# Top-32 attention and two rational/cosine layers: the mask moved to ScalarE, two elementwise steps moved to VectorE

## The chip, the cores and the metric

The kernel runs on one core of a Trainium2 chip. The metric is the device time of one execution in microseconds (us). TensorE multiplies matrices, VectorE, ScalarE and GpSimd work elementwise, SyncE issues transfers. In profile rows TensorE is PE (its weight loads PEld), VectorE is DVE, ScalarE ACT, GpSimd POOL, SyncE SP.

## The reference, cut to what matters

Attention with 4 batches, 8 heads, 576 positions and 64 features per head. Of each row of scores only the 32 largest are kept. Then two layers over 2304 tokens (512 wide, 2048 inside) follow, the first with a rational function, the second with h cos(h). All is in float32.

```
kth  = 32nd largest of the row of scores
attn = exp(where(scores >= kth, scores, -1e9) - max)
attn = attn / (sum(attn) + 1e-9);  x = attn @ v
h = x @ w_in                                # first layer
P = a0 + a1 h + a2 h^2 + a3 h^3;  Q = 1 + |b0| |h| + |b1| h^2
x = (P / (Q + 1e-6)) @ w_out
h = x @ w_in2;  out = (h * cos(h)) @ w_out2 # second layer
```

## The kernel before, in words

**Units.** Attention is cut into 72 units: 18 query tiles of 128 rows times 4 pairs of heads. `qk(i)` multiplies queries by keys on TensorE into the PSUM tile `sx` and ScalarE copies the scores of both heads to SBUF (`sS`, two buffers). `topk(i)` finds the 32 largest on VectorE: it folds each row into element-wise maxima and minima of its two halves (tile `e`, two buffers), then takes eight maxima at a time (`hd`, MAX8) and strikes them out (MATCH_REPLACE8), four rounds in all, the first two on the maxima alone. ScalarE scales the negated row maximum (`nb`), and forms exp(SCALE * score + nb) for all scores, into `e`. Last, VectorE multiplies by the mask score >= hd[31] and sums the row as it goes, the sum into `sums`. `av(i)` transposes `e` on TensorE (tiles `pp`, copied to SBUF as `pt` by ScalarE) and multiplies by the values; `norm` scales by the reciprocal sums once four units of a tile are done.

**Matrix stages.** The tokens come in 9 blocks of 256; block k needs the 8 units of query tiles 2k and 2k+1. Each of the two layers has 8 groups per block, 72 in all. `in1` multiplies by the first weights (`mm_in`, into PSUM tile `h`), copies to `w`, and starts the rational function on ScalarE and GpSimd: `u` = -(a3 w + a2) on ScalarE, then u * w on GpSimd. `mid1` and `end1` finish on VectorE, `out1` multiplies by the second weights into `y`. For the second layer `in2` copies `h` to `hs`, forms `rr` = hs/2pi + 1/4, adds the constant MAGIC (which rounds to an integer, into `n`, a tile on the single buffer "ob" that the output rows also use), subtracts to get the fraction, and takes the sine of two groups in one ScalarE instruction. The sine needs another activation table than the exponential and the logarithm, so a table is loaded before and after it. `mul2` and `out2` follow. Operands are split in a high and a low part, so that each product is three multiplications. The weights are converted and split in the first part of the run (`conv`), among the attention.

**Order.** `attention()` is a generator of five pieces per unit. A loop over pieces starts it and calls the matrix stages' functions at piece numbers worked out ahead (`timed`). The framework then orders the instructions of each engine with a simulated timeline, tied by a window of pieces for VectorE, ScalarE and GpSimd (`Windowed`, line 70), up to piece 150, 90 and 90. On the chip each engine works in that order. Nearly all elementwise instructions are issued through `Windowed`, so their line in the profile is L79, and the tile's name tells them apart. The PSUM pools for `h`, `y`, `o` and the transposes have one buffer each. `DV1` = 8 and `DV2` = 7 are the blocks from which some steps of GpSimd and ScalarE go to VectorE instead.

The lines that decide the mask's place are, in `topk`:

```
for j, s in enumerate(tiles):
    top(j, both, 3)
    A.activation(e[:, j], s, AF.Exp, bias=nb[:, j:j + 1], scale=SCALE)
yield
...
V.scalar_tensor_tensor(e[:, j], s, hd[j][:, 31:32], e[:, j],
                       op0=ALU.is_ge, op1=ALU.mult, accum_out=row)
```

In the next unit's first piece the loop takes two steps of the generator of the unit before, which are these masks, and then calls `av(i - 1)`.

Of the kernel before, what the change touches and what calls it, by code (L numbers as in the profile page):

```python
# [10 lines left out]
F32 = mybir.dt.float32  # L11
# [3 lines left out]
AF = mybir.ActivationFunctionType  # L15
ALU = mybir.AluOpType
# [7 lines left out]
P = 128  # L24
# [3 lines left out]
SCALE = 0.125  # L28
HALF = S // 2
NEG = -3.0e38  # L30
VW = 640
TWO_PI = 6.283185307179586
MAGIC = 12582912.0
SSC = TWO_PI
# [15 lines left out]
NC0 = 36  # L50
C2 = 80
PM = 150
PMASK = range(0)
WA, PA = 12, 90
WG, PG = 10, 90
N1, NU, N2, NST, NGG = 2, 2, 3, 4, 3
# [32 lines left out]
def body(tc, out, qt, kt, vt, ident_d, w1_d, w1o_d, a_d, b_d, w2_d, w2o_d):  # L89
    nc = tc.nc  # L90
    V, A, G = Windowed(tc, nc.vector, WIN, PM), Windowed(tc, nc.scalar, WA, PA), Windowed(tc, nc.gpsimd, WG, PG)
    PE, SP = nc.tensor, nc.sync

    with ExitStack() as ctx:
        def pool(name, bufs=1, **k):
            return ctx.enter_context(tc.tile_pool(name=name, bufs=bufs, **k))

        cst = pool("cst")
# [3 lines left out]
        sml = pool("sml", 4)  # L102
# [25 lines left out]
        sx = ps_s.tile([P, 2, 512], F32, name="sx")  # L128
# [51 lines left out]
        def load_v(i):  # L180
# [4 lines left out]
            for j, (b, _) in enumerate(qts[n]):  # L185
                v = kv.tile([P, VW], F32, tag="v", bufs=VB, name=f"v{i}_{b}")
                A.dma_start(out=v, in_=vt[b, pr])
# [14 lines left out]
        V.tensor_scalar_mul(nega, coef[:, 0:4], -1.0)  # L202
        quarter = cst.tile([P, 1], F32)
        G.memset(quarter, 0.25)
        magic = cst.tile([P, 1], F32)
        G.memset(magic, MAGIC)
        qc = cst.tile([P, 1], F32)
        G.memset(qc, QC)
        tc.keep_in_program_order(A.preload_act_table_set("natural_log_exp_and_others"))
        na0, na1, na2, na3 = (nega[:, i:i + 1] for i in range(4))  # L210
# [68 lines left out]
        def halves(ap):  # L279
            return ap.rearrange("p (a c) -> p a c", a=2)  # L280

        def after(mm, bank):
            for x in order[bank]:
                tc.add_manual_dep(mm.ins, x, mybir.DependencyInfo(mybir.DependencyClass.NoSync, mybir.DependencyReason.DATA), reason="bank")

        def qk(i):
            n, pr = units[i]
            raw, hi, lo = (*qpair[i // 2], None, None)[:3]
            kvs = ins[i]
            m = P // len(kvs)  # L290
            st[i] = sb = att.tile([P, 2, S], F32, tag="sS", bufs=2, name=f"sS{i}")
            for j in range(2):
                rows = slice(j * D, (j + 1) * D)
                for c, (k, _) in reversed(list(enumerate(kvs))):
                    q0 = i % 2 * P
                    qs, qc = slice(0, (c + 1) * m), slice(q0, q0 + (c + 1) * m)
                    for hf in range(2):
                        o = sx[qs, hf, :HALF]
                        hs = slice(hf * HALF, (hf + 1) * HALF)
                        if n < 2:  # L300
                            mm = PE.matmul(o, raw[rows, j, qc], k[rows, 0, hs].bitcast(F32), start=True, stop=True)
                            after(mm, hf)
                        else:
                            mm = PE.matmul(o, hi[:, j, qc], k[:, j, hs], start=True, stop=False, skip_group_check=True)
                            after(mm, hf)
                            mm = PE.matmul(o, lo[:, j, qc], k[:, j, hs], start=False, stop=True, skip_group_check=True)
                        order[hf] = [mm.ins.name]
                A.activation(halves(sb[:, j]), sx[:, :, :HALF], AF.Copy)
            if n == 1:
                store_k(kvs[0][0], 0, pr)  # L310

        def topk(i):
            n, pr = units[i]
            sc = st.pop(i)
            tiles = [sc[:, j] for j in range(2)]
            e = att.tile([P, 2, S], F32, tag="e", bufs=EB, name=f"e{i}")
            et[i] = e
            kb, t = n // 2, n % 2
            if i % 8 == 0:
                sums[kb] = sml.tile([P, 2, H], F32, tag="sum", bufs=2, name=f"sum{kb}")  # L320
            sm = sums[kb][:, t]
            hds = sml.tile([P, 2, 32], F32, tag="hd", bufs=2, name=f"hd_{i}")
            hd = [hds[:, j] for j in range(2)]
            nb = sml.tile([P, 2], F32, tag="nb", bufs=2, name=f"nb_{i}")
            big = [e[:, j, :HALF] for j in range(2)]
            both = [e[:, j] for j in range(2)]

            def top(j, x, r):
                V.max(out=hd[j][:, 8 * r:8 * r + 8], in_=x[j])

            def drop(j, x, r):
                V.match_replace(out=x[j], in_to_replace=hd[j][:, 8 * r:8 * r + 8], in_values=x[j], imm_value=NEG)

            l, r = sc[:, :, :HALF], sc[:, :, HALF:]
            V.tensor_tensor(e[:, :, :HALF], l, r, op=ALU.max)
            top(0, big, 0)
            yield
            V.tensor_tensor(e[:, :, HALF:], l, r, op=ALU.min)
            top(1, big, 0)
            A.activation(nb, hds[:, :, 0], AF.Copy, scale=-SCALE)  # L340
            yield
            for step in (((drop, big, 0), (top, big, 1)), ((drop, big, 1), (top, both, 2)), ((drop, both, 2),)):
                for f, *x in step:
                    for j in range(2):
                        f(j, *x)
                yield
            for j, s in enumerate(tiles):
                top(j, both, 3)
                A.activation(e[:, j], s, AF.Exp, bias=nb[:, j:j + 1], scale=SCALE)
            yield  # L350
            for j, s in enumerate(tiles):
                row = sm[:, 2 * pr + j:2 * pr + j + 1]
                if i in PMASK:
                    G.tensor_scalar(s, s, hd[j][:, 31:32], 1.0, op0=ALU.is_ge, op1=ALU.mult)
                    G.tensor_mul(e[:, j], e[:, j], s)
                    A.activation(s, e[:, j], AF.Copy, accum_out=row)
                else:
                    V.scalar_tensor_tensor(e[:, j], s, hd[j][:, 31:32], e[:, j], op0=ALU.is_ge, op1=ALU.mult, accum_out=row)
                yield

        def av(i):
# [89 lines left out]
        def in1(k, g):  # L451
            h = mm_in(0, k, g).rearrange("p a t -> p (a t)")
            w, q, r, u = (mo.tile([P, BT * 2], F32, tag="m1" + t, bufs=NU if t == "u" else N1, name=f"{t}{k}_{g}") for t in "wqru")
            A.activation(w, h, AF.Copy)
            A.activation(r, w, AF.Abs)
            A.activation(q, r, AF.Identity, scale=b1, bias=b0)
            E1 = V if k >= DV1 else G
            E1.tensor_mul(q, q, r)
            A.activation(r, q, AF.Ln, bias=qc)
            A.activation(r, r, AF.Exp, scale=-1.0)  # L460
            A.activation(u, w, AF.Identity, scale=na3, bias=na2)
            E1.tensor_mul(u, u, w)
            g1[k, g] = (q, r, u, w)

# [52 lines left out]
        def in2(k, g):  # L517
            h = mm_in(1, k, g).rearrange("p a t -> p (a t)")
            if g % SINB == 0:
                rp[k, g // SINB] = late[0].tile([P, SINB, 512], F32, tag="rr", bufs=2, name=f"rr{k}_{g}")  # L520
            rs = rp[k, g // SINB]
            rr = rs[:, g % SINB]
            hs = late[0].tile([P, 512], F32, tag="hs", bufs=N2, name=f"hs{k}_{g}")
            rt[k, g] = rr, hs
            A.activation(hs, h, AF.Copy)
            n = late[0].tile([P, DM], F32, tag="ob", bufs=OBB, name=f"n{k}_{g}")
            if k >= DV2:
                V.tensor_scalar(rr, hs, 1.0 / TWO_PI, 0.25, op0=ALU.mult, op1=ALU.add)
            else:
                A.activation(rr, hs, AF.Identity, scale=1.0 / TWO_PI, bias=quarter)  # L530
            A.activation(n, rr, AF.Identity, bias=magic)
            V.scalar_tensor_tensor(rr, n, MAGIC, rr, op0=ALU.subtract, op1=ALU.subtract)
            if g % SINB == SINB - 1:
                A.activation(rs, rs, AF.Sin, scale=-SSC)
                if k < NB - 1:
                    tc.keep_in_program_order(A.preload_act_table_set("natural_log_exp_and_others"))

# [103 lines left out]
        def attention():  # L641
            load_k(1)
            load_v(0)
            qk(0)
            prev = None
            nrm, fresh, held = [], [], []
            for i in range(nu + 1):
                if LQ == 0 and i % 2 == 0 and i + 2 < nu:
                    load_q(i + 2)
                if i + 1 < nu:  # L650
                    qk(i + 1)
# [57 lines left out]
def _layout(q, k, v, moe_w_in, moe_w_out, moe_a, moe_b, moe2_w_in, moe2_w_out):  # L709
# [9 lines left out]
    vp = v.reshape(B, NP, 2, S, D)  # L719
    vh = np.zeros((B, NP, P, VW), np.float32)  # L720
    vh[..., :512] = vp[:, :, :, :512].reshape(B, NP, 2, 4, P, D).transpose(0, 1, 4, 3, 2, 5).reshape(B, NP, P, 512)
# [19 lines left out]
```

## Time and profile before

| | |
|---|---|
| time, median of 3 runs | 1469.39 us (1466.33 to 1470.24) |
| profiled execution | 1473.49 us, span 1471.7 us |
| busy TensorE | 1270.3 us, 86% of the span |
| busy VectorE | 1283.4 us, 87% |
| busy ScalarE | 1082.1 us, 74% |
| busy GpSimd | 680.4 us, 46% |
| HBM traffic | 213 GB/s over the span |
| granted TensorE clock, mean | 0.92 of full speed |

The span is the time from the first to the last instruction of the profiled execution. Busy shares are means over stages that have different limits. The chain that ended last is followed back from the last instruction: at each step to what released it, or to the instruction before it on the same engine. A duration in a row includes the time in which an instruction that has started is held by something that engines share.

### The profile page before, as it was taken

To read this page: it belongs to the slowest core of one execution; us is meant where nothing else is said; L and a number is where in the kernel's file an instruction comes from. 1 tells how busy PE (TensorE), PEld (TensorE's weight loads), DVE (VectorE), ACT (ScalarE), POOL (GpSimd) and SP (SyncE) were. 2 spreads that over 40 slices of the span, in tenths; PEclk is the share of its full clock that TensorE was granted. 3 is DMA by queue.
4 is the path that set the end of the run, shared out by engine and by line. 5 is a ranking of instruction groups with operands and counts; after the bars stand their busy time and mean duration, and the time that the engine had idled before them with its cause. 6 is when DMAs were issued, how large, how long until landed. Compare 5 with 4: busy or idle time off the path is not lost.

```text
span 1471.7 us, 25059 instructions
## 1 busy us (share of the span) xinstructions
PE 1270.3 (86%) x9016; PEld 1120.9 (76%) x9016; DVE 1283.4 (87%) x2477; ACT 1082.1 (74%) x1873; POOL 680.4 (46%) x503
## 2 busy tenths in 40 slices
PE   5766787657898799989988998999999899999988
PEld 2434565546896698889888997888899799988986
DVE  6999999789999999989989999999999999745533
ACT  5777778665787678778877877878878577876643
POOL 3879466654354346335544644444545344420000
PEclk9677798757999899999999999999999999999999
DMA  7886756775456656555765665565467677656677
GB/s 227 286 280 209 238 183 201 239 229 197 136 190 200 208 183 211 190 175 205 241 221 176 219 212 190 182 215 198 176 219 247 215 253 260 226 196 226 233 239 230
DMA packets 141549, 314.98 MB, mean 214 GB/s; under 512 B 12016, under 2 KB 28528, under 8 KB 141424
## 3 DMA queue, kind: packets, MB, share of 16 engines
q1 hardware_dynamic: 122832, 261.99, 53.4%
q10 hardware_dynamic: 18592, 51.39, 10.4%
q8 instruction: 71, 1.16, 0.3%
q14 instruction: 54, 0.44, 0.1%
HBM read 278.20 MB, written 35.13 MB: 213 GB/s over the span
## 4 chain that ended last, share of the span: by engine, by line
DVE 37%; PE 28%; ACT 13%; DMA 11%; issue 6%; POOL 5%; SPq 0%; ACTq 0%; POOLq 0%; DVEq 0%
DVE e L79 17%; DVE hd L79 8%; PE o L558 6%; DVE u L79 5%; PE h L444 4%; PE h L446 4%; PE h L445 4%; DVE cb L79 2%; POOL cb L79 2%; PE y L503 2%; PE y L502 2%; ACT L79 2%; DMA raw<-w 2%; DMA w1ol<-w1ol 2%; PE y L501 2%
## 5 line engine op out<-in xcount | busy, mean ns | idle before, releaser
L79 DVE MAX8 hd<-e 128x8 f32<-128x288 f32 (+1 forms) x576 | 322.3, 592 | 0.0
L558 PE MATMUL o<-w2o,gg 128*128 128x512 f32 x864 | 233.8, 409 | 9.7 <-DMA w2o<-w2o 8.5
L79 DVE MATCH_REPLACE8 e<-hd,e 128x288 f32<-128x288 f32 (+1 forms) x432 | 230.2, 537 | 0.0
L558 PEld LDWEIGHTS o<-w2o,gg 128*128 128x128 f32 x864 | 160.6, 197 | 40.5 <-DMA w2o<-w2o 9.9
L79 DVE TENSOR_TENSOR e<-sS 128x576 f32<-128x576 f32 x144 | 166.9, 1196 | 24.9 <-ACT sS L79 15.2
L444 PE MATMUL h<-xh,w1hi 128*128 128x256 f32 x576 | 171.6, 298 | 12.5 <-ACT hs L79 6.3
L502 PE MATMUL y<-gg,w1o 128*128 128x256 f32 x576 | 169.3, 294 | 6.7 <-POOL gg L79 6.6
L445 PE MATMUL h<-xl,w1hi 128*128 128x256 f32 x576 | 167.6, 291 | 6.8 <-DVE xl L79 6.8
L501 PE MATMUL y<-gg,w1o 128*128 128x256 f32 x576 | 169.2, 294 | 4.6 <-ACT gg L79 4.6
L79 POOL TENSOR_TENSOR gg<-u,gg 128x512 fp32r<-128x512 f32 x64 | 91.8, 1435 | 174.5 <-ACT gg L79 158.8
L444 PE MATMUL h<-x2h,w2hi 128*128 128x256 f32 x576 | 165.9, 288 | 5.2 <-ACT w L79 2.7
L503 PE MATMUL y<-gg,w1ol 128*128 128x256 f32 x576 | 167.8, 291 | 1.6 <-DMA w1ol<-w1ol 1.5
L446 PE MATMUL h<-x2h,lo 128*128 128x256 f32 x576 | 164.9, 286 | 3.2 <-DMA lo<-w2lo 3.2
L446 PE MATMUL h<-xh,lo 128*128 128x256 f32 x576 | 166.4, 289 | 0.0
L445 PE MATMUL h<-x2l,w2hi 128*128 128x256 f32 x576 | 164.5, 286 | 2.1 <-DVE x2l L79 2.1
L79 DVE SCALAR_TENSOR_TENSOR e<-sS,hd,e 128x576 f32<-128x576 f32 x144 | 151.7, 1068 | 16.4 <-ACT e L79 16.2
L79 POOL TENSOR_TENSOR u<-u,w 128x512 f32<-128x512 f32 x64 | 91.8, 1435 | 157.3 <-ACT u L79 148.9
L79 POOL TENSOR_TENSOR rr<-rr,hs 128x512 f32<-128x512 f32 x56 | 78.2, 1418 | 127.7 <-ACT rr L79 127.7
L79 ACT ACTIVATE e<-sS,nb 128x576 f32<-128x576 f32 x144 | 107.9, 772 | 29.8 <-DVE hd L79 29.5
L444 PEld LDWEIGHTS h<-xh,w1hi 128*128 128x128 f32 x576 | 113.4, 197 | 18.1 <-ACT hs L79 8.4
L502 PEld LDWEIGHTS y<-gg,w1o 128*128 128x128 f32 x576 | 113.9, 198 | 10.9 <-POOL gg L79 9.0
L501 PEld LDWEIGHTS y<-gg,w1o 128*128 128x128 f32 x576 | 114.3, 198 | 9.1 <-ACT gg L79 7.5
(1167 smaller groups left out, 3793.1 us busy)
## 6 DMA issues: line engine op xcount, KB each, us to landing
w2o<-w2o SPq DMA_DIRECT2D x144, 512.0 KB, 4.2
lo<-w1lo SPq DMA_DIRECT2D x72, 512.0 KB, 4.0
w1ol<-w1ol SPq DMA_DIRECT2D x72, 512.0 KB, 3.8
lo<-w2lo SPq DMA_DIRECT2D x72, 512.0 KB, 4.4
k<-kdr ACTq DMA_DIRECT2D x44, 576.0 KB, 5.0
raw<-w SPq DMA_DIRECT2D x32, 512.0 KB, 4.6
v<-vt ACTq DMA_DIRECT2D x48, 320.0 KB, 3.7
qr<-qt ACTq DMA_DIRECT2D x36, 256.0 KB, 4.0
```

Of the source, the lines that this page charges most:

```text
L79: r = f(*a, **k)
L444: PE.matmul(h[:, i, :], wh, xh[:, c, :], start=(c == 0), stop=False)
L445: PE.matmul(h[:, i, :], wh, xl[:, c, :], start=False, stop=False)
L446: PE.matmul(h[:, i, :], lo[:, i, c, :], xh[:, c, :], start=False, stop=(c == NCC - 1))
L501: PE.matmul(y[:, c, :], w1o[:, f, cs], gh[:, i, :], start=(f == 0 and c % 2 == 0), stop=False, skip_group_check=True)
L502: PE.matmul(y[:, c, :], w1o[:, f, cs], gl[:, i, :], start=False, stop=False, skip_group_check=True)
L503: PE.matmul(y[:, c, :], wl[:, i, cs], gh[:, i, :], start=False, stop=(f == NF - 1), skip_group_check=True)
L558: PE.matmul(o[:, t, :], l[:, i, ts], wt[i][:, r], start=(f == 0 and r == 0 and l is gh), stop=(f == NF - 1 and l is gl), skip_group_check= ...
```

## The change

`topk` no longer masks on VectorE. The scores are scaled by 1/8 as they are copied out of PSUM. When the 32nd largest value t is known, ScalarE negates it (`nt`), and applies Prelu to score - t with a slope of 2^120 below zero: kept scores stay as they are, and others become hugely negative. A one-column instruction forms `nb` = t - max, and the exponential of the result plus `nb` goes to `e`; its row sum is taken by the accumulator of ScalarE. This is done for each of the two heads in turn. The exponential no longer stands before the mask, and the copy of the row maximum after the first MAX8 is dropped. The first step of the cubic, `u`, goes from ScalarE to VectorE as a tensor-scalar. In `in2` the rounding becomes one VectorE tensor-scalar that adds MAGIC and subtracts it again, and the subtraction becomes a tensor-tensor with the sign turned, so that the sine's scale turns its sign too.

```diff
--- before.py
+++ after.py
@@ -28,6 +28,7 @@
 SCALE = 0.125
 HALF = S // 2
 NEG = -3.0e38
+STEEP = 2.0 ** 120
 VW = 640
 TWO_PI = 6.283185307179586
 MAGIC = 12582912.0
@@ -50,7 +51,6 @@
 NC0 = 36
 C2 = 80
 PM = 150
-PMASK = range(0)
 WA, PA = 12, 90
 WG, PG = 10, 90
 N1, NU, N2, NST, NGG = 2, 2, 3, 4, 3
@@ -202,8 +202,6 @@
         V.tensor_scalar_mul(nega, coef[:, 0:4], -1.0)
         quarter = cst.tile([P, 1], F32)
         G.memset(quarter, 0.25)
-        magic = cst.tile([P, 1], F32)
-        G.memset(magic, MAGIC)
         qc = cst.tile([P, 1], F32)
         G.memset(qc, QC)
         tc.keep_in_program_order(A.preload_act_table_set("natural_log_exp_and_others"))
@@ -305,14 +303,13 @@
                             after(mm, hf)
                             mm = PE.matmul(o, lo[:, j, qc], k[:, j, hs], start=False, stop=True, skip_group_check=True)
                         order[hf] = [mm.ins.name]
-                A.activation(halves(sb[:, j]), sx[:, :, :HALF], AF.Copy)
+                A.activation(halves(sb[:, j]), sx[:, :, :HALF], AF.Copy, scale=SCALE)
             if n == 1:
                 store_k(kvs[0][0], 0, pr)
 
         def topk(i):
             n, pr = units[i]
             sc = st.pop(i)
-            tiles = [sc[:, j] for j in range(2)]
             e = att.tile([P, 2, S], F32, tag="e", bufs=EB, name=f"e{i}")
             et[i] = e
             kb, t = n // 2, n % 2
@@ -322,6 +319,7 @@
             hds = sml.tile([P, 2, 32], F32, tag="hd", bufs=2, name=f"hd_{i}")
             hd = [hds[:, j] for j in range(2)]
             nb = sml.tile([P, 2], F32, tag="nb", bufs=2, name=f"nb_{i}")
+            nt = sml.tile([P, 2], F32, tag="nt", bufs=2, name=f"nt_{i}")
             big = [e[:, j, :HALF] for j in range(2)]
             both = [e[:, j] for j in range(2)]
 
@@ -337,25 +335,21 @@
             yield
             V.tensor_tensor(e[:, :, HALF:], l, r, op=ALU.min)
             top(1, big, 0)
-            A.activation(nb, hds[:, :, 0], AF.Copy, scale=-SCALE)
             yield
             for step in (((drop, big, 0), (top, big, 1)), ((drop, big, 1), (top, both, 2)), ((drop, both, 2),)):
                 for f, *x in step:
                     for j in range(2):
                         f(j, *x)
                 yield
-            for j, s in enumerate(tiles):
+            for j in range(2):
                 top(j, both, 3)
-                A.activation(e[:, j], s, AF.Exp, bias=nb[:, j:j + 1], scale=SCALE)
             yield
-            for j, s in enumerate(tiles):
-                row = sm[:, 2 * pr + j:2 * pr + j + 1]
-                if i in PMASK:
-                    G.tensor_scalar(s, s, hd[j][:, 31:32], 1.0, op0=ALU.is_ge, op1=ALU.mult)
-                    G.tensor_mul(e[:, j], e[:, j], s)
-                    A.activation(s, e[:, j], AF.Copy, accum_out=row)
-                else:
-                    V.scalar_tensor_tensor(e[:, j], s, hd[j][:, 31:32], e[:, j], op0=ALU.is_ge, op1=ALU.mult, accum_out=row)
+            for j in range(2):
+                if j == 0:
+                    A.activation(nt, hds[:, :, 31], AF.Copy, scale=-1.0)
+                A.activation(e[:, j], sc[:, j], AF.Prelu, bias=nt[:, j:j + 1], alpha=STEEP)
+                A.activation(nb[:, j:j + 1], hd[j][:, 0:1], AF.Identity, scale=-1.0, bias=hd[j][:, 31:32])
+                A.activation(e[:, j], e[:, j], AF.Exp, bias=nb[:, j:j + 1], accum_out=sm[:, 2 * pr + j:2 * pr + j + 1])
                 yield
 
         def av(i):
@@ -458,7 +452,7 @@
             E1.tensor_mul(q, q, r)
             A.activation(r, q, AF.Ln, bias=qc)
             A.activation(r, r, AF.Exp, scale=-1.0)
-            A.activation(u, w, AF.Identity, scale=na3, bias=na2)
+            V.tensor_scalar(u, w, na3, na2, op0=ALU.mult, op1=ALU.add)
             E1.tensor_mul(u, u, w)
             g1[k, g] = (q, r, u, w)
 
@@ -528,10 +522,10 @@
                 V.tensor_scalar(rr, hs, 1.0 / TWO_PI, 0.25, op0=ALU.mult, op1=ALU.add)
             else:
                 A.activation(rr, hs, AF.Identity, scale=1.0 / TWO_PI, bias=quarter)
-            A.activation(n, rr, AF.Identity, bias=magic)
-            V.scalar_tensor_tensor(rr, n, MAGIC, rr, op0=ALU.subtract, op1=ALU.subtract)
+            V.tensor_scalar(n, rr, MAGIC, -MAGIC, op0=ALU.add, op1=ALU.add)
+            V.tensor_sub(rr, rr, n)
             if g % SINB == SINB - 1:
-                A.activation(rs, rs, AF.Sin, scale=-SSC)
+                A.activation(rs, rs, AF.Sin, scale=SSC)
                 if k < NB - 1:
                     tc.keep_in_program_order(A.preload_act_table_set("natural_log_exp_and_others"))
```

## Rows read from the trace of the kernel before

**Rows 1.** Windows of four stretches: length, busy us (instructions) by engine, granted clock.
```profile
0.00:400.00 400.00, 274.57 (x1409) 202.43 (x1410) 362.93 (x664) 280.36 (x518) 245.74 (x201) 0.77 0.68 221
400.00:1200.00 800.00, 740.58 (x5711) 683.75 (x5710) 759.41 (x1539) 626.19 (x1089) 382.61 (x264) 0.97 0.61 204
1200.00:1280.00 80.00, 78.39 (x693) 73.87 (x693) 74.45 (x142) 63.74 (x108) 36.29 (x27) 1.00 0.73 250
1280.00:1471.00 191.00, 176.71 (x1209) 160.88 (x1207) 86.65 (x135) 111.80 (x161) 15.78 (x12) 0.99 0.68 226
```

**Rows 2.** The page's chain that ended last: shares of the span by engine.
```profile
DVE 37%; PE 28%; ACT 13%; DMA 11%; issue 6%; POOL 5%; SPq 0%; ACTq 0%; POOLq 0%; DVEq 0%
```

**Rows 3.** The chain by line, 0 to 400 us, then 400 to 1280 us.
```profile
by line: DVE e L79 15.6%; DVE cb L79 8.5%; issue 8.5%; POOL cb L79 7.4%; DVE hd L79 6.8%; DMA raw<-w 6.3%; DMA raw<-w2o 4.1%; DMA w2lo<-cb 2.8%; DVE u L79 2.7%; DMA w2o<-cb 2.1%; ACT cb L79 1.9%; DMA w1ol<-w1ol 1.8%; POOL raw L79 1.8%; PE h
by line: DVE e L79 21.6%; DVE hd L79 10.3%; DVE u L79 7.9%; issue 5.3%; PE o L558 4.6%; PE h L444 3.3%; PE h L445 3.2%; PE h L446 3.2%; ACT L79 2.9%; DVE rr L79 2.3%; DVE q L79 2.3%; ACT e L79 1.9%; ACT r L79 1.8%; PE sx L392 1.7%; ACT rr L
```

**Rows 4.** Groups by form, VectorE, 0 to 400 us: xcount, busy us, mean ns.
```profile
L79 DVE SCALAR_TENSOR_TENSOR e<-sS,hd,e 128x576 f32<-128x576 f32 x38 | 43.9, 1160 | 1.2 <-ACT e L79 1.2
L79 DVE SCALAR_TENSOR_TENSOR u<-u,nega,w 128x512 f32<-128x512 f32 x12 | 11.7, 974 | 3.0 <-POOL u L79 3.0
```

**Rows 5.** Groups by form, VectorE, 400 to 1280 us.
```profile
L79 DVE SCALAR_TENSOR_TENSOR e<-sS,hd,e 128x576 f32<-128x576 f32 x106 | 107.8, 1035 | 15.1 <-ACT e L79 14.9
L79 DVE SCALAR_TENSOR_TENSOR u<-u,nega,w 128x512 f32<-128x512 f32 x51 | 65.3, 1280 | 8.7 <-POOL u L79 8.7
L79 DVE SCALAR_TENSOR_TENSOR rr<-n,rr 128x512 f32<-128x512 f32 x51 | 40.8, 800 | 0.1
```

**Rows 6.** Groups by form, VectorE, whole span.
```profile
L79 DVE DVE_READ_ACCUMULATOR e<-sS,hd,e 128x1 f32 x144 | 11.1, 77 | 0.0
L79 DVE TENSOR_SCALAR rs<-sum 128x8 f32<-128x8 f32 x18 | 9.0, 501 | 0.1
L79 DVE TENSOR_SCALAR rr<-hs 128x512 f32<-128x512 f32 x16 | 6.8, 425 | 26.7 <-ACT hs L79 26.7
L79 DVE TENSOR_TENSOR rr<-rr,hs 128x512 f32<-128x512 f32 x16 | 10.3, 689 | 8.3 <-ACT rr L79 8.3
```

**Rows 7.** The tile views of e and rs: ns min/median/max, first and last start.
```profile
L79 DVE SCALAR_TENSOR_TENSOR e<-sS,hd,e x144: 790/808/1914, 27.4 to 1272.5; 128x576 f32<-128x576 f32 x144
L79 DVE TENSOR_SCALAR rs<-sum x18: 145/165/1300, 82.8 to 1273.3; 128x8 f32<-128x8 f32 x18
```

**Rows 8.** The timeline, ScalarE, near 704 and 711 us: start, duration, idle before.
```profile
704.01 0.80 ACT L79 ACTIVATE u<-w,nega 128x512 f32<-128x512 f32 x1
...
704.72 0.26 ACT L79 ACTIVATE xs<-sx 128x128 f32<-128x128 f32 x1
...
710.98 0.73 ACT L79 ACTIVATE n<-rr,magic 128x512 f32<-128x512 f32 x1 [0.83 <-DMA out<-ob]
711.61 1.43 ACT L79 ACTIVATE e<-sS,nb 128x576 f32<-128x576 f32 x2
712.94 0.62 ACT L79 ACTIVATE qh<-qr 128x512 fp32r<-128x512 f32 x1
```

**Rows 9.** Groups by form, ScalarE, whole span.
```profile
L79 ACT ACTIVATE e<-sS,nb 128x576 f32<-128x576 f32 x144 | 107.9, 772 | 29.8 <-DVE hd L79 29.5
L79 ACT ACT_TABLE_LOAD x67 | 86.0, 1283 | 3.4 <-issue 2.1
L79 ACT ACTIVATE nb<-hd 128x2 f32<-128x2 f32 x72 | 14.5, 201 | 52.9 <-DVE hd L79 52.2
```

**Rows 10.** The waits, whole span: us in total, times, longest.
```profile
DVE e L79 <- ACT e L79: 16.2, 15, 3.0
ACT e L79 <- DVE hd L79: 29.5, 29, 2.8
```

**Rows 11.** The chain in order of time, around 707 us.
```profile
706.77 4.18 DMA out<-ob
```

**Rows 12.** The timeline, VectorE, at 1443 us.
```profile
1443.50 0.69 DVE L79 SCALAR_TENSOR_TENSOR rr<-n,rr 128x512 f32<-128x512 f32 x1 [0.79 <-ACT n L79]
```

## Prediction

> **What bounds the kernel now.** I read the windows first, by stage. From 0 to 400 us, while the weights are split into high and low halves, VectorE is busy 362.93 of 400 us, TensorE only 274.57. From 400 to 1280 us attention and both matrix stages run together: VectorE 759.41 + 74.45 = 833.9 of 880 us (95%), TensorE 819.0 (93%), ScalarE 689.9 (78%). After 1280 us attention is over and VectorE falls to 86.65 of 191 us [rows 1]. So VectorE is fullest for 1280 us, but TensorE, at 78.39 of 80 us just before that point, can hardly be fuller than 98%, and is near it. Then the chain: VectorE holds 37% of it, TensorE 28%, ScalarE 13%, DMA 11% [rows 2]. By stage VectorE's listed lines are e, cb, hd and u, 15.6 + 8.5 + 6.8 + 2.7 = 33.6% in the first, and e, hd, u, rr and q, 21.6 + 10.3 + 7.9 + 2.3 + 2.3 = 44.4% in the second [rows 3]. Where VectorE is busy 95% and holds 44% of the chain, 0.47 of each microsecond saved on it lands on the end by this reading; in the first stage 33.6 / 90.7 = 0.37.
>
> **Off VectorE: the mask.** 144 masking instructions go, each with its read of the accumulator. In the first stage 38 of them cost 43.9 us, and the reads 38 x 0.077 = 2.9: 46.8 us [rows 4, 6]. In the second 106 cost 107.8 + 8.2 = 116.0 us [rows 5, 6]. That is by the mean (1.16 and 1.04 us); the median is 0.808 us [rows 7], the rest being waits on something that VectorE shares, and if those waits pass to the next instruction the saving is 106 x 0.885 = 93.8 us in the second stage. VectorE's waits for the exponential go too, 16.2 us in all [rows 10], 1.2 and 14.9 of them by stage [rows 4, 5].
>
> **Onto VectorE: two short instructions and a swap.** Per group of the first matrix stage (72) one tensor-scalar for the cubic's first step, per group of the second (72) one for the rounding. The only row of that kind and size is rr<-hs, 0.425 us, run late when GpSimd is almost idle (15.78 of 191 us) [rows 1, 6]. What GpSimd adds is seen on rs<-sum: 8 columns, 0.165 us at the median, 0.501 in the mean, 1.300 at most [rows 6, 7]. So 0.336 us is added in the mean: 0.76 us each. In the second stage 51 + 51 of them: 77.6 us; in the first 12 (u alone counts there): 9.1. Bounds for the second stage: 102 x 0.425 = 43.4, and 102 x (0.425 + 1.135) = 159 if each is held as the worst rs was. The subtraction that replaces the rounding's scalar-tensor-tensor has a near row, rr<-rr,hs with 0.689; the old one takes 0.800 in the second stage with its waits, and with the same waits the new one costs the same [rows 5, 6]: 0, between -6 and 0 us. VectorE's net is then -46.8 + 9.1 - 1.2 = -39 us in the first stage and -116.0 + 77.6 - 14.9 = -53 in the second; from the bounds the second could be -88 to +65.
>
> The Trainium skill (SBUF — State Buffer, Who interferes with whom) says that VectorE and GpSimd share a port pair that is locked for a whole instruction, by a VectorE instruction with two SBUF inputs or in its two-port form, tensor-scalar among them, and the loser is blocked until the end. The trace agrees: the 8-column rs takes up to 1.300 us. By that rule a GpSimd instruction that meets no mask any more meets the next two-input instruction, which speaks for the lower saving, and for the second rival below.
>
> **Onto ScalarE.** No row shows Prelu. The nearest is the exponential itself, same shape, a column as bias: 0.772 us, 1.33 from start to start for two [rows 8, 9]; bounds 0.62 (a 512-column copy) and 0.81 (u, two pointer columns) [rows 8]. Per unit: two Prelu at 0.665 (1.33); two one-column nb at 0.201 [rows 9], in full, because the exponential waits for them (0.40; 0 if hidden); nt for the old nb (0); the accumulator reads, which no ScalarE row shows, as on VectorE, 2 x 0.077 (0.15; 0.4 at nb's price); and each exponential now reads what Prelu just wrote, so that the overlap 0.772 - 0.665 is lost, twice (0.21). Sum 2.1 us per unit, 1.2 to 2.9. Off ScalarE go n, 0.63 from start to start (710.98 to 711.61), and u, 0.71 (704.01 to 704.72) [rows 8]. First stage: 19 x 2.1 - 12 x 0.71 = +31 us, 280 to 311 of 400. Second: 53 x 2.1 - 51 x 1.34 = +43, to 733 of 880, 83%. ScalarE's listed chain lines are 1.9% against 70% busy in the first stage and 2.9 + 1.9 + 1.8 = 6.6% against 78% in the second [rows 1, 3], so 0.03 and 0.08 land: +1 and +4 us.
>
> The Trainium skill (ScalarE: Activation LUTs, What ACT_TABLE_LOAD costs) gives 186 ns plus 0.833 per column and 93 ns for a pointer operand, so 0.28 us for nb. The nb row, without a pointer bias, has 0.201. By the page the sum would be some 11 us higher on ScalarE, about 1 on the end.
>
> **Waits that are added.** nt now stands on ScalarE behind the last of the four maxima, with two heads of Prelu, nb and exponential behind it, and PSUM evictions (w, hs, pt, xs) behind those. The exponentials wait there already, 29.5 us in all [rows 10]; I add nothing, and the rival below prices it. The rounding's result n lies in the single buffer that it shares with the output: ScalarE has stood until an output DMA of 4.18 us had read it [rows 11], 0.83 us of it idle [rows 8]. Now VectorE would stand there, with the top-32 work behind it: 0, and up to 8 x 4.2 x 0.47 = 16 us. The norm's sums come from ScalarE instead of VectorE, 18 times: 0, because the first addition that needs them comes a unit after most of them. In the tail the rounding loses one hop, the 0.79 us that rr waits for n [rows 12], once on the end: -1.
>
> **The sum.** 0.37 x -39 = -14; 0.47 x -53 = -25; ScalarE +5; tail -1: **-35 us**. On the profiled execution (1473.49 us, 1471.7 of it span) that is 1438.5; the median of the runs is 1469.39, 4.1 below the profiled one: **1435 us**, since VectorE's whole saving can't land where TensorE is at 93% beside it. If the share is off by a third the gain is 20 to 50: 1420 to 1450.
>
> **Rivals.**
> *VectorE sets the pace alone.* Then its saving lands whole until TensorE is the bound: the first stage gives 39; the second at most 819.0 - 880 x 0.98, that is, it shrinks from 880 to 819.0 / 0.98 = 836, 44 us. 1469.4 - 83 = 1386. For it: VectorE's 95%, and that its own waits are few. Against it: chain shares of 34 and 44%, and DMA and GpSimd in the first stage's chain. 0.15.
> *The tensor-scalars eat the saving.* Masks are worth only their median, 0.885 with the read, and each tensor-scalar is held as u<-u,nega,w is, 1.280 against 0.689 alone [rows 5, 6], so 1.02 us. First stage -33.6 + 12.2, times 0.37 = -8; second -93.8 + 103.5 - 14.9, times 0.47 = -2; ScalarE +5: -5, 1464 to 1465, just at the edge of what can be told. For it: rs at 1.3 us; against it: rounding comes where GpSimd is busy 48% only. 0.13.
> *ScalarE's queue holds TensorE back: slower.* From nt to the second exponential ScalarE is tied up for some 3.9 us per unit where two exponentials took 1.43, 2.4 more, and evictions of single-buffered PSUM tiles stand behind. TensorE's slack is 61 us of 880, 1.2 per unit: it turns slower when more than half of the 2.4 falls on a needed eviction. With three quarters: (1.8 - 1.2) x 53 = +32, less 14 of the first stage: +18, 1487. For it: one buffer each for h, pt, o and y, VectorE's chain meeting ScalarE's; against it: ScalarE has 17% left. 0.25.
> *Prelu is not in the loaded table.* The table loads stand at 1.283 us each [rows 9]; two a unit are 72 x 2.57 = 185 us more on ScalarE, which then is the bound in the second stage, 733 + 136 of 880 and in order: about 1469 + 120 = 1590. The Trainium skill (ScalarE: Activation LUTs, Table sets: the hidden batching unit) names relu, copy, identity and abs as in every set, and Prelu not; no run here shows it. 0.02.
>
> **How the numbers follow.** The forecast has 0.45. Timing tells 0.3% (4.4 us) from no change. Faster: 0.44 of the forecast, 0.15, 0.05 of the second rival and 0.01 of the third: 0.65. Same: 0.01 + 0.06 + 0.02 = 0.09. Slower: 0.02 + 0.22 + 0.02 = 0.26. The range leaves out the far ends of the first and third rival and the fourth: 1398 to 1486.
>
> **What would show it.** Right: no masks on VectorE, its busy time in 400 to 1280 us lower by about 40 us; the new tensor-scalars at 0.7 to 0.8 us in the mean; Prelu near 0.77; ScalarE at 83% there; the number of table loads unchanged; units closer together by 3%. Wrong: TensorE waiting for w, hs or pt in place of VectorE's share (third rival); tensor-scalars over 1 us (second); a first stage as long as before, because DMA and GpSimd set it.

## The result, and the profile after

The changed kernel took 1480.92 us (median of 8; 1475.65 to 1487.15) against 1469.82 us of the kernel before (median of 8): a ratio of 1.0071, 95% interval 1.0044 to 1.0099. It is 11 us slower, clear of the 0.3% that can be told. The profiled execution took 1480.59 us, its span is 1478.8. One execution of all that follow, of the run with the late exponential, was slower at a lower granted clock (0.805 instead of about 0.93), and its median leaves that one out.

The windows of the kernel after, columns as in [rows 1] (TensorE, its weight loads, VectorE, ScalarE, GpSimd):

```profile
0.00:400.00 400.00, 277.50 (x1510) 208.57 (x1511) 338.89 (x629) 313.23 (x640) 242.61 (x206) 0.81 0.69 225
400.00:1200.00 800.00, 724.10 (x5554) 664.92 (x5553) 699.33 (x1386) 634.50 (x1253) 364.28 (x257) 0.97 0.61 200
1200.00:1280.00 80.00, 76.31 (x658) 71.71 (x658) 70.00 (x142) 62.31 (x117) 35.26 (x26) 1.00 0.73 247
1280.00:1471.00 191.00, 182.66 (x1295) 166.43 (x1294) 105.62 (x177) 102.14 (x152) 20.74 (x15) 1.00 0.71 235
```

VectorE's busy time fell as it should: 362.93 to 338.89 us in the first stage, 759.41 to 699.33 in the next 800 us, where the mean granted clock is the same 0.97. But no other engine became fuller there by as much. TensorE's busy time fell too, 740.58 to 724.10, and GpSimd's; ScalarE's rose by 8. The chain that ended last, by engine, answers [rows 2]:

```profile
PE 27%; DVE 27%; ACT 15%; DMA 5%; issue 4%; POOL 4%; ACTq 0%; POOLq 0%; DVEq 0%
```

These shares add up to 82% only, because this chain could be followed back no further than 250 us into the span, while that of [rows 2] starts at 1 us; so the two rows can't be set side by side. From 400 to 1280 us, which both chains cover whole, all lines of VectorE together hold 39% instead of 46%, ScalarE's 21% instead of 17%, TensorE's 28% instead of 25%.

The stage of the loss shows on two marks, the first transposes of units 18 and 71 (ns min/median/max, then first and last start). Before:

```profile
L374 PE MATMUL pp18a<-ident,e x4: 272/273/273, 391.2 to 391.5; 128*128 128x128 f32 x4
L374 PE MATMUL pp71a<-ident,e x4: 272/273/328, 1277.2 to 1277.5; 128*128 128x128 f32 x4
```

and after:

```profile
L368 PE MATMUL pp18a<-ident,e x4: 273/273/331, 378.6 to 379.0; 128*128 128x128 f32 x4
L368 PE MATMUL pp71a<-ident,e x4: 272/272/327, 1291.8 to 1292.2; 128*128 128x128 f32 x4
```

Unit 18 comes 12.6 us earlier, and from it to unit 71 the kernel before takes 886.0 us, the changed one 913.2: 27.2 us lost while attention and both matrix stages run together. After unit 71 it gains 7.5 (1471.7 - 1277.2 = 194.5 against 1478.8 - 1291.8 = 187.0). -12.6 + 27.2 - 7.5 = +7.1, the difference of the spans. Each mark comes from one execution, and executions of one kernel differ by some 5 us either way.

What VectorE got, groups by form of the whole span (the first two are the instructions of [rows 5], which has them from 400 to 1280 us alone):

```profile
L79 DVE SCALAR_TENSOR_TENSOR u<-u,nega,w 128x512 f32<-128x512 f32 x72 | 82.1, 1140 | 19.0 <-POOL u L79 18.6
L79 DVE TENSOR_TENSOR rr<-rr,n 128x512 f32<-128x512 f32 x72 | 55.6, 772 | 0.7
L79 DVE TENSOR_SCALAR u<-w,nega 128x512 f32<-128x512 f32 x72 | 51.2, 711 | 37.7 <-ACT w L79 37.6
L79 DVE TENSOR_SCALAR n<-rr 128x512 f32<-128x512 f32 x72 | 35.7, 495 | 9.0 <-DMA out<-ob 6.4 <-ACT rr L79 2.2
```

What ScalarE got, which answers [rows 9]:

```profile
L79 ACT ACTIVATE e<-e,nb 128x576 f32<-128x576 f32 x144 | 110.5, 771 | 0.0
L79 ACT ACTIVATE e<-sS,nt 128x576 f32<-128x576 f32 x144 | 103.6, 767 | 0.1
L79 ACT ACT_TABLE_LOAD x67 | 86.0, 1283 | 3.3 <-issue 2.1
L79 ACT ACTIVATE nb<-hd 128x1 f32<-128x1 f32 x144 | 41.5, 289 | 33.8 <-DVE hd L79 32.1 <-POOL ql L79 1.2
L79 ACT ACTIVATION_READ_ACCUMULATOR e<-e,nb 128x1 f32 x144 | 28.1, 195 | 0.0
```

The table loads are 67 as before: Prelu needs none of its own. And where VectorE stands now, from the waits of 400 to 1280 us (us, times, longest), after:

```profile
DVE e L79 <- ACT sS L79: 28.9, 13, 5.4
DVE u L79 <- ACT w L79: 28.3, 10, 7.6
DVE q L79 <- ACT r L79: 9.3, 9, 2.9
```

and the rows of the kernel before for two of them in the same stretch (the third did not exist there, as u was ScalarE's):

```profile
DVE e L79 <- ACT sS L79: 7.5, 7, 3.1
DVE q L79 <- ACT r L79: 1.9, 3, 0.9
```

These three rose from 9.4 to 66.5 us, while VectorE's wait for the exponential, 14.9 us there [rows 5], is gone. By itself this does not show the loss: an engine that has less to do waits more. TensorE has the same work in both kernels. From unit 18 to 71 it is idle 61.0 us before and 80.9 after, and its waits for ScalarE, all rows of the view added up, rise from 37.2 to 56.2 us. The largest of matrix stages before:

```profile
PE h L444 <- ACT hs L79: 4.6, 6, 1.1
PE h L444 <- ACT w L79: 2.2, 2, 1.7
PE y L501 <- ACT gg L79: 0.9, 3, 0.5
```

and after:

```profile
PE h L438 <- ACT w L79: 9.7, 9, 2.0
PE h L438 <- ACT hs L79: 7.1, 9, 2.7
PE y L495 <- ACT gg L79: 4.4, 5, 2.5
```

One of VectorE's waits in the timeline of the kernel after (start, duration), on VectorE:

```profile
671.70 0.69 DVE L79 TENSOR_TENSOR rr<-rr,n 128x512 f32<-128x512 f32 x1
674.08 1.46 DVE L79 TENSOR_TENSOR e<-sS 128x576 f32<-128x576 f32 x1 [1.70 <-ACT sS L79]
```

the last product of these scores on TensorE:

```profile
669.18 0.29 PE L304 MATMUL sx<-k,ql 128*128 128x288 f32 x1
```

and ScalarE in the same microseconds:

```profile
670.29 1.43 ACT L79 ACTIVATE e<-sS,nt 128x576 f32<-128x576 f32 x2
...
671.62 0.62 ACT L79 ACTIVATE gg<-u 128x512 fp32r<-128x512 f32 x1
672.15 0.76 ACT L79 ACTIVATE e<-e,nb 128x576 f32<-128x576 f32 x1
672.81 0.18 ACT L79 ACTIVATION_READ_ACCUMULATOR e<-e,nb 128x1 f32 x1
672.90 0.61 ACT L79 ACTIVATE qh<-qr 128x512 fp32r<-128x512 f32 x1
673.43 0.62 ACT L79 ACTIVATE sS<-sx 128x576 f32<-128x576 f32 x1
```

VectorE has finished the unit before and stands 1.70 us for the next scores, sS. The copy of sS on ScalarE started at 673.43 with no idle time ahead of it: in front of it stood two Prelu, an exponential and an accumulator read (2.1 us of the mask, start to start), and gg and qh. TensorE had the scores ready at 669.47, so they stood 3.96 us in ScalarE's queue. Of the 13 waits for sS, 12 look like this: the scores had been ready for 1.8 to 7.2 us when ScalarE began to copy them.

### The profile page after: what moved, and what is told of

It is laid out like the page before. It is cut to its first block, busy times and chain, and to the rows that moved or that the text cites. A ratio compares the mean times of both kernels' runs of the same rounds, so it can differ in the third digit from the quotient of the medians.

```text
span 1478.8 us, 25235 instructions
## 1 busy us (share of the span) xinstructions
PE 1262.4 (85%) x9016; PEld 1112.8 (75%) x9016; DVE 1214.7 (82%) x2333; ACT 1112.9 (75%) x2161; POOL 662.9 (45%) x502
## 4 chain that ended last, share of the span: by engine, by line
PE 27%; DVE 27%; ACT 15%; DMA 5%; issue 4%; POOL 4%; ACTq 0%; POOLq 0%; DVEq 0%
DVE e L79 10%; DVE hd L79 7%; PE o L552 6%; DVE u L79 5%; PE h L438 4%; PE h L440 4%; PE h L439 4%; ACT e L79 3%; ACT L79 3%; PE y L497 2%; DMA w2o<-w2o 2%; PE y L496 2%; PE y L495 2%; ACT r L79 2%; ACT rr L79 1%
## 5 line engine op out<-in xcount | busy, mean ns | idle before, releaser
L552 PE MATMUL o<-w2o,gg 128*128 128x512 f32 x864 | 225.5, 399 | 13.0 <-DMA w2o<-w2o 12.9
L552 PEld LDWEIGHTS o<-w2o,gg 128*128 128x128 f32 x864 | 154.9, 190 | 45.8 <-DMA w2o<-w2o 15.1
L438 PE MATMUL h<-xh,w1hi 128*128 128x256 f32 x576 | 168.4, 292 | 20.0 <-ACT hs L79 8.7
L79 POOL TENSOR_TENSOR u<-u,w 128x512 f32<-128x512 f32 x64 | 87.7, 1371 | 126.6 <-DVE u L79 118.0
L438 PEld LDWEIGHTS h<-x2h,w2hi 128*128 128x128 f32 x576 | 111.1, 193 | 18.1 <-ACT w L79 12.5
L496 PEld LDWEIGHTS y<-gg,w1o 128*128 128x128 f32 x576 | 113.6, 197 | 12.6 <-POOL gg L79 10.9
L79 POOL TENSOR_TENSOR q<-q,r 128x512 f32<-128x512 f32 x64 | 90.6, 1416 | 69.2 <-ACT q L79 60.7
```

The lines of the kernel that those rows point to most:

```text
L79: r = f(*a, **k)
L438: PE.matmul(h[:, i, :], wh, xh[:, c, :], start=(c == 0), stop=False)
L496: PE.matmul(y[:, c, :], w1o[:, f, cs], gl[:, i, :], start=False, stop=False, skip_group_check=True)
L552: PE.matmul(o[:, t, :], l[:, i, ts], wt[i][:, r], start=(f == 0 and r == 0 and l is gh), stop=(f == NF - 1 and l is gl), skip_group_check= ...
```

## The experiments

Fifteen kernels, each beside the kernel before on the same chip; ratio with its 95% interval. "Unit 18" and "18 to 71" are the marks above, in each run's profiled execution (before: 391.2 and 886.0).

**The parts by themselves.** The kernel before with one or two parts of the change.

```diff
  # m: the new topk() and the scaled copy of the scores only
  # u:
-A.activation(u, w, AF.Identity, scale=na3, bias=na2)
+V.tensor_scalar(u, w, na3, na2, op0=ALU.mult, op1=ALU.add)
  # r:
-A.activation(n, rr, AF.Identity, bias=magic)
-V.scalar_tensor_tensor(rr, n, MAGIC, rr, op0=ALU.subtract, op1=ALU.subtract)
+V.tensor_scalar(n, rr, MAGIC, -MAGIC, op0=ALU.add, op1=ALU.add)
+V.tensor_sub(rr, rr, n)
  # mu: m and u
```

The mask only:

> Mask on ScalarE alone; u and the rounding stay on ScalarE. Theory Q (ScalarE's queue: the mask chain of some 4 us a unit holds back the score copies and evictions, so VectorE idles): slower than before by 10 to 30 us, as ScalarE's busy time rises by about 180 us to 1260; VectorE's wait for sS over 40 us in all. Theory H (head of the line: it is the moved u, which on VectorE stands waiting for w with the top-32 work behind it): faster than before or equal, 1445 to 1470, and VectorE's waits for ScalarE small. Theory P (the planner only dealt another order, worth about half a per cent either way): anything within 10 us of before.

Measured 1486.92 us, 1.0124 (1.0101 to 1.0148). The page's busy line (us, share of the span, instructions) has VectorE 140 us below before and ScalarE 118 above:

```profile
PE 1276.0 (86%) x9016; PEld 1121.7 (76%) x9016; DVE 1143.0 (77%) x2189; ACT 1199.9 (81%) x2305; POOL 665.1 (45%) x503
```

It is slower than the full change. So the loss is in the mask, not in u's wait: theory H falls, as the main cause. Theory Q had the time, and VectorE's wait for the scores (61.9 us from 400 to 1280 us), but it expected 60 us more of ScalarE's busy time than came.

The cubic's step only:

> Only the cubic's first step moves to VectorE. Theory H: slower than before by 10 us or more, VectorE's wait u<-w about 35 us. Theory Q: within 5 us of before or up to 15 slower by VectorE's 51 us more work, with ScalarE's waits fewer. Theory P: within 10 us.

1502.16 us, 1.0213 (1.0186 to 1.0239). The wait u<-w is 16.6 us in all, half of what H asked for; the rest is VectorE's work, 1343.6 against 1283.4 us busy. The time rises by 31 us for 60 us of work. Neither Q nor P had that.

The rounding only:

> Only the rounding moves to VectorE. All theories: near before; VectorE has 36 us more, ScalarE 52 less: 0 to +12 us by the chain's share. Theory H would also see VectorE wait for the output DMA that reads the shared buffer, some 6 us in all.

1498.23 us, 1.0191 (1.0165 to 1.0218): 28 us for 34 us of VectorE's work (1317.3 busy). No theory foresaw that much. In the kernel before VectorE's added work costs 0.5 to 0.8 us per us, although ScalarE loses some 45 us of busy time in each of the two runs.

Mask and cubic's step:

> Mask and cubic's step moved, rounding left on ScalarE. Theory Q: slower than the full change (ScalarE 52 us busier), 1480 to 1500. Theory H: as the full change, 1475 to 1485, since the wait u<-w stays. Theory P: within 10 us of the full change either way.

1478.86 us, 1.0067 (1.0047 to 1.0087), level with the full change (1.0071), as H and P had it and Q not. With the mask on ScalarE, moving u off it gives some 8 us, and the rounding nothing that can be told.

**What VectorE's saving is worth.**

```diff
-V.scalar_tensor_tensor(e[:, j], s, hd[j][:, 31:32], e[:, j], ..., accum_out=row)
+   # nothing; the sums are set to a constant
```

> Leaves out the mask and the row sums (the sums are set to a constant); all else as before. VectorE loses its 163 us and ScalarE gains nothing: what VectorE's saving is worth by itself. Theory S (the saving is worth what the chain's share says, and ScalarE's added work ate it): 1400 to 1425, i.e. 45 to 70 us below before. Theory T (VectorE's saving is worth little after 400 us, since TensorE and the loop through all engines bind there): 1445 to 1465, VectorE's idle time up by over 100 us. Theory P (the planner's order is what counts): 1450 to 1480.

1423.54 us, 0.9695 (0.9668 to 0.9721). Unit 18 at 364.2, 27 us earlier; from there to unit 71 858.0 us, 28 less. So the whole saving, free of ScalarE's price, is worth some 47 us. That is in theory S's range, but the two shares of the prediction would give 79 (0.37 x 48 + 0.47 x 131). VectorE is busy 1137.0 us, and TensorE's lines hold 59% of the chain from 400 to 1280 us. The windows view from unit 18 to 71 (length, TensorE, weight loads, VectorE, ScalarE, GpSimd, clock):

```profile
364.20:1222.20 858.00, 817.73 (x6501) 760.30 (x6499) 741.04 (x1491) 697.16 (x1209) 414.22 (x298) 0.99 0.65 216
```

VectorE's wait for the scores there, and TensorE's largest wait for ScalarE (us, times, longest):

```profile
DVE e L79 <- ACT sS L79: 26.1, 17, 5.6
PE sx L304 <- ACT sS L79: 6.9, 6, 3.9
```

TensorE is busy 817.7 of 858 us there, and waits for ScalarE 15.7 us in all: by these rows and the chain it is the next bound, which keeps the rest of VectorE's saving from landing. VectorE waits here as long for sS as in the full change (26.1 against 28.9 us), in a kernel that is 57 us faster.

**ScalarE's load or the dependence.** The same kernel with the change's ScalarE work but nobody waiting for it:

```diff
+A.activation(s, s, AF.Prelu, alpha=2.0, bias=nb[:, j:j + 1])     # in place, after the exponential
+A.activation(dm[:, j:j + 1], hds[:, j, 0:1], AF.Identity, scale=-1.0, bias=nb[:, j:j + 1])
-A.activation(e[:, j], s, AF.Exp, bias=nb[:, j:j + 1], scale=SCALE)
+A.activation(e[:, j], s, AF.Exp, bias=nb[:, j:j + 1], scale=SCALE, accum_out=dm[:, 2 + j:3 + j])
```

> Leaves out mask and row sums as d1 does, and adds the change's ScalarE work, two Prelu, two one-column instructions and two accumulator reads a unit, for which nothing waits (Prelu works in place on the spent scores). ScalarE's busy time should rise by about 150 us over d1's 1078. Theory L (ScalarE's added time, in its one queue, ate the saving): d1's 1424 plus 30 to 60, 1454 to 1484. Theory C (it is the dependence: the exponential now comes after the last maximum and Prelu): 1424 to 1440.

1479.85 us, 1.0064 (1.0045 to 1.0083): 56 us above the kernel without a mask, for 125 us more of ScalarE's busy time (1203.7 against 1078.5). Theory L had 30 to 60. From unit 18 to 71 it takes 910.7 us, nearly the 913.2 of the full change. The same two views, the windows:

```profile
377.90:1288.60 910.70, 831.72 (x6499) 769.28 (x6497) 743.61 (x1489) 791.47 (x1531) 415.98 (x299) 0.97 0.61 204
```

and the waits:

```profile
DVE e L80 <- ACT sS L80: 43.1, 21, 4.3
PE y L499 <- ACT gg L80: 10.9, 6, 2.8
PE sx L305 <- ACT xs L80: 6.8, 4, 2.7
PE h L442 <- ACT w L80: 6.8, 7, 2.7
```

VectorE has the same work as in the kernel without a mask, and waits 17 us longer for the scores alone. TensorE has the same work too, and is idle 79.0 us instead of 40.3; its waits for ScalarE, all rows added up, rise from 15.7 to 47.0 us. So the queue holds back both. The planner dealt both kernels an order of their own, which the runs below put at 5 us, and in one stage at up to 17.

Without mask and row sums too, with the same number of instructions, but nb is made from the last maximum of both heads, and the exponentials stand a step later in the program:

```diff
-A.activation(nb, hds[:, :, 0], AF.Copy, scale=-SCALE)            # after the first maxima
 ...
+A.activation(nb, hds[:, :, 31], AF.Copy, scale=-SCALE)           # after the last, in the mask's place
 A.activation(e[:, j], s, AF.Exp, bias=nb[:, j:j + 1], scale=SCALE)
```

> Leaves out mask and row sums as d1 does, and lets the exponential wait for the 32nd value (its bias is the negated 32nd value instead of the maximum), with as many ScalarE instructions as d1. Theory L: 1420 to 1434, as d1. Theory C: 1450 or more.

1442.1 us, 0.9808 (0.9787 to 0.9829): 19 us for the dependence, between the two theories. What it adds is less than the expectation says. The exponential overwrites the tile `e` that the maxima are read from, and in the kernel without a mask too all 144 start after the last maximum of their own head, 0.9 us after it at the median; here it is 2.5 us, as they wait for both heads and for nb. The small nb after the first maxima is gone as well, which alone may be a gain (see the kernel before without the maximum). The 19 us lie in the first stage: unit 18 at 380.8 instead of 364.2, but 861.9 from there to unit 71. So both cost; the load costs three times as much, and it, not the dependence, is what is lost in the second stage (52.7 against 3.9 us).

**Without the maximum.** The full change:

```diff
-A.activation(nb[:, j:j + 1], hd[j][:, 0:1], AF.Identity, scale=-1.0, bias=hd[j][:, 31:32])
-A.activation(e[:, j], e[:, j], AF.Exp, bias=nb[:, j:j + 1], accum_out=...)
+A.activation(e[:, j], e[:, j], AF.Exp, accum_out=...)
```

> The full change without the row maximum: the exponential of score - t needs none, so the 144 one-column nb go from ScalarE (41.5 us busy, and the wait of the exponential behind them). Theory S: 10 to 20 us faster than the full change, 1460 to 1470. Theories T and P: within 6 us of the full change.

1469.35 us, 0.9997 (0.9974 to 1.0020): 11 us below the full change, as S said, for 34 us less of ScalarE (1079.4 busy), and level with the kernel before. The mask alone without the maximum:

> Mask alone on ScalarE in all units, no maximum; u and rounding left on ScalarE. L at 0.37 us per us of ScalarE's work: 1487 less 0.37 x 42 = 1471, so level with the full change without the maximum (1469), that is, u and the rounding pay nothing back. If the mask's cost lies in ScalarE's fullness alone: 1475 or more, because ScalarE is still some 1155 us busy against 1079 there. P: 1465 to 1485.

1487.81 us, 1.0127 (1.0100 to 1.0153), level with the mask alone. Of the three expectations only that by ScalarE's fullness holds. So u and the rounding do pay back, 18 us, once the maximum is gone, where they paid 6 with it. ScalarE, busy 1167.3 us here, gave nothing for the 33 us that it lost: a saving on it does not land evenly.

The kernel before without the maximum:

```diff
-A.activation(nb, hds[:, :, 0], AF.Copy, scale=-SCALE)
-A.activation(e[:, j], s, AF.Exp, bias=nb[:, j:j + 1], scale=SCALE)
+A.activation(e[:, j], s, AF.Exp, scale=SCALE)
```

> The kernel before without the row maximum in the exponential (which these small scores do not need): 72 small ScalarE instructions (14.5 us) and the wait of 52 us for the first maxima go, and the exponential waits for no maximum. If ScalarE's queue matters even where VectorE is the fullest (L): 5 to 12 us faster, 1458 to 1465. C: within 5 us of before. P: anywhere within 15 us.

1453.45 us, 0.9885 (0.9869 to 0.9900): 17 us faster than before, for 22 us less busy ScalarE (1060.4). That is more than any theory had. Among the kernels that keep the mask and the sums it is the fastest here. The gain lies in the first stage: unit 18 comes at 373.5, 17.7 us earlier, and from there to unit 71 it takes 883.3 us, 2.7 less. The small nb stood in ScalarE's queue until VectorE's first maxima came, 52.2 us in all [rows 9], with everything else behind it. The exponential's own wait for the maxima rises in return, from 29.5 to 44.6 us, and it takes 0.681 us instead of 0.772, as it has no column for a bias. Which of these gave the 17 us isn't told apart. It holds for scores as small as these, where the exponential needs no maximum. The mark of unit 18 and the exponential, of this run:

```profile
L372 PE MATMUL pp18a<-ident,e x4: 272/273/328, 373.5 to 373.9; 128*128 128x128 f32 x4
L79 ACT ACTIVATE e<-sS 128x576 f32<-128x576 f32 x144 | 96.4, 681 | 45.2 <-DVE hd L79 44.6
```

**Fewer units.** Mask on ScalarE (without the maximum) in units 0 to 19, and in every third:

```diff
+AMASK = range(20)          # or range(0, 72, 3)
+if i in AMASK:
+    A.activation(nb, hds[:, :, 31], AF.Copy, scale=-SCALE)      # once per unit
+    A.activation(e[:, j], s, AF.Prelu, bias=nb[:, j:j + 1], scale=SCALE, alpha=STEEP)
+    A.activation(e[:, j], e[:, j], AF.Exp, accum_out=row)
```

> Mask on ScalarE without the maximum for units 0 to 19 only; those after, the cubic's step and the rounding as before. In the full change unit 18 came 12.6 us earlier. Theory S and T: that lead is kept, 1452 to 1460. Theory P: it is lost again by another order, 1463 to 1478.

1463.00 us, 0.9949 (0.9930 to 0.9967). Unit 18 comes at 371.7, 19.5 us earlier, of which 7 are left at the end: theory P's edge, not the lead kept of S and T. Most of the lead need not be the mask's: the kernel before without the maximum, with every mask on VectorE, has unit 18 at 373.5. From unit 18 to 71 the time is 896.9 us, 10.9 more than before, though from unit 20 on the instructions are the same.

> Mask on ScalarE without the maximum in every third unit; the others, the cubic's step and the rounding as before. VectorE loses some 54 us, ScalarE gains some 43 to 50. Theory S: the work is split nearer to where both are full, 1445 to 1462. Theory T: 1460 to 1470. Theory P: 1463 to 1480.

1487.58 us, 1.0123 (1.0092 to 1.0154): worse than none and than all. Unit 18 comes at 394.5, later than before. None of the theories foresaw it, and why stays open; the mixed units may have made a poor order, which was not tried.

> Mask on ScalarE for units 0 to 19 as in the run with the first units, and no maximum in any unit. If ScalarE's queue (L) is what both spare: about 1446 (7 below the kernel before without the maximum, 1453). If order decides (P): 1446 to 1465.

1469.25 us, 0.9997 (0.9980 to 1.0013). That is neither theory's time. The two gains are nearly one and the same, the first stage without the maximum: unit 18 comes at 370.5 here, 371.7 with the first units and 373.5 without the maximum alone. But from there to unit 71 this run takes 900.1 us, against 883.3 without the maximum alone, though from unit 20 on the instructions are the same. Why stays open.

**Order alone.** The kernel before, and the full change, with

```diff
-WIN = 8
+WIN = 9
```

> The kernel before with VectorE's window of pieces 9 instead of 8: the same instructions, another order from the planner up to piece 150. Theory P (order alone moves this kernel as much as the change did): over 7 us away from before, either way. Theories L and C: within 5 us.

1464.20 us, 0.9969 (0.9949 to 0.9988), 5 us, between the theories.

> The full change with VectorE's window of pieces 9 instead of 8: order only. The same step moved the kernel before by -0.3%. If the loss of 0.7% is the change's and not the order's: 1474 to 1487 (within 0.4% of the full change). If order makes the sign: 1470 or less, or over 1490.

1479.56 us, 1.0069 (1.0042 to 1.0097). Another order of the same instructions moved one kernel by 0.3% and the other not at all. So the sign of the 0.7% holds in both orders; but differences of 5 us between two kernels with different order should not be given a cause, and the runs with the first units show a stage that takes 11 and 17 us longer with nearly the same instructions. The 53 us of ScalarE's load from unit 18 to 71 are far beyond that; the 19 us of the dependence are not.

## Why the prediction was wrong

**The step that failed is the landing of the second stage: "0.47 x -53 = -25" with "ScalarE +5".** In its place stands +27.2 us from unit 18 to unit 71. Three terms of it were wrong:

1. *ScalarE's price, 0.03 and 0.08 per us.* With 125 us of ScalarE work for which nothing waits, the time rose by 56 us, 0.45 per us of busy time. I read the price off ScalarE's share of the chain, and misread that: [rows 3] list only the longest lines, and ScalarE's work is spread over some forty short ones. All its lines hold 16.9% of the chain from 400 to 1280 us, not 6.6%; the 13% of [rows 2] is 191 us, against 66 in the lines that I added up. By the prediction's own rule the price is then 0.22 per us, still half of what was measured: I did not ask what else stands in ScalarE's one queue. It is the way by which scores, h and transposes leave PSUM, so that its delay becomes VectorE's wait for scores and TensorE's wait for free tiles and operands; TensorE's rises from 15.7 to 47.0 us by the load alone, and from 37.2 to 56.2 between the kernel before and the one after. That is the third rival, which I gave 0.25: its sign, TensorE waiting for w, hs and pt, came true (20 us more idle in the stage, where it had 32), and its 1487 us is the nearest of all to the 1481 measured.
2. *VectorE's share, 0.47.* The mask taken away altogether shortened the second stage by 28 us, for 131 us that I counted there (116.0 and the wait of 14.9): 0.21. In the first stage it was 27 us for 48, 0.56 instead of 0.37. Adding work to VectorE costs 0.5 to 0.8. The chain's share is the price of none of these: with VectorE's work less, TensorE is at 817.7 of 858 us.
3. *The dependence, priced at 0.* "The exponentials wait there already": true, all 144 start after the last maximum of their head. But one that waits for both heads and a small nb besides costs some 19 us, nearly all in the first stage. No run has Prelu's result as all that is added to wait for.

The three runs give -47 + 56 + 19 = +28 us for the mask; the mask alone measured +18, so the parts do not simply add up.

**What held.** The first stage: -14 forecast, -12.6 measured, but by luck: it is made of larger parts that cancel (27 gained by VectorE, 14 to 17 lost to load or dependence), and the old nb, priced at 0, may be worth up to 17 us there. The tail: -1 forecast, -7.5 measured. Prelu at 0.767 us against 0.772 taken. The tensor-scalars were 0.711 us for u and 0.495 for the rounding, 1.21 together against 1.52, so VectorE's busy time fell by 69 us, where the forecast's terms give 53 (162.8 of masks less 144 x 0.76); the second rival is out. nb takes 0.289 us, against 0.201 taken, and the accumulator read 0.195 against 0.077. The Trainium skill (ScalarE: Activation LUTs, What ACT_TABLE_LOAD costs) gives about 0.28 us for a one-column activation with a pointer bias; the trace agrees. ScalarE's busy time rose by 31 us in all, less than the 72 x (2.1 - 1.34) = 55 of the forecast, because ScalarE's instructions overlap (in the timeline above the exponential starts at 672.15, before gg ends at 672.24): their durations, added up, rise by 70 us. It is not the amount that failed but its price. u's move brought a wait that was not in the sum, 28.3 us behind w in the second stage, and the rounding one of 6.4 us behind the output DMA, within its bound.

Left open: why every third unit is worse than all; why the second stage takes 11 to 17 us longer behind a first stage that is masked on ScalarE; and how much of the 17 us without the maximum is the wait, and how much the work that goes.

## What to carry to other kernels

A share of the chain of waits is not a price: it misjudged a saving (0.21 for 0.47) and an added load (0.45 for 0.08) alike. An engine with many short instructions is also easily undercounted in a list of the chain's longest lines; take its share by engine. Before moving work from the fullest engine to one with 20% to spare, look at what else stands in the second engine's queue and who waits for it, above all the copies out of single-buffered PSUM tiles; and try the added load alone, with nobody waiting, as it is a small experiment. Read the waits of an engine whose work did not change: those of an engine that lost work rise in any case. Look also at small instructions that wait for another engine in a full queue: dropping one of 0.2 us per unit, and the exponential's bias with it, gave 17 us.

## What the runs showed of the hardware

A ScalarE accumulator read takes 0.195 us, a one-column activation with a pointer bias (a column in memory) 0.289, a two-column one without 0.201. An exponential over 576 columns takes 0.772 us with a pointer bias and 0.681 without. A tensor-scalar over 512 columns had in the changed kernel a median of 0.545 us with two pointer scalars and 0.418 with two constants. Prelu with an alpha of 2^120 over 576 columns takes 0.767 us, the exponential behind it 0.771, and it needs no table load of its own: 67 loads before and after.
